# Gates of chunks 1 to 5 on 80 partitions, with the running maximum copied there by DMA

## The chip, the cores and the metric

The kernel runs on one core of a Trainium2 chip. The core has a matrix engine (TensorE, PE in the profile, with weight loads shown as PEld), a vector engine (VectorE, DVE), an engine for activation functions (ScalarE, ACT), a general engine (GpSimd, POOL) and a queue processor (SyncE, SP) that issues the DMA transfers here. The engines run side by side and wait for one another through semaphores. The metric is the time of one execution on the device in microseconds (us); less is better.

## The reference

Three layers follow one another: a gated linear attention with a stabilised recurrence, a feed-forward layer with a smooth relu, and a soft mixture of eight experts whose weights are normalised in eight rounds. The change lies in the gates of the first:

```python
for t in range(S):                                   # S = 768, for each of 2 batches and 8 heads
    m_new = maximum(f_gate[t] + m, i_gate[t])        # running maximum, m starts at -1e30
    f_stab = exp(f_gate[t] + m - m_new)
    i_stab = exp(i_gate[t] - m_new)
    m = m_new
    C = f_stab * C + i_stab * outer(v[t], k[t])
    n = f_stab * n + i_stab * k[t]
    h = C @ q[t];  nq = n . q[t]
    y[t] = sigmoid(o_gate[t]) * h / max(|nq|, 1)
# x = y as 1536 tokens x 320
# layer 2: g = smooth relu of x @ w_in (320 x 2048); x = g @ w_out
# layer 3: P = exp(x @ w_gate - max), 8 rounds of row and column normalisation;
#          out = sum over 8 experts of P[:, e] * (relu(x @ w1[e]) @ w2[e])
```

All is float32; the kernel splits operands into a high and a low part for the matrix engine.

## The kernel before

The sequence is cut into 6 chunks of 128 tokens; with 2 batches there are 12 attention tiles, tile t being chunk t // 2 of batch t % 2. Within a chunk the recurrence is written as matrices. For that the gates are needed in three forms: the stabilised f along the tokens (G, spread to all 128 partitions), the stabilised i and the running product of f by token (gt), and each chunk's whole product (lend).

The gates stand in one tile g_all on 32 partitions (batch and head, held twice), with i, f and the running maximum m along 768 columns. `gate_exps(a, b)` makes the running maximum by one scan (line 306), then f + m - m_new (309, 310) and i - m_new (312) on DVE and the exponentials on ACT (311, 313). It is called for columns 0 to 128 and then for 128 to 768. `gate_prods` makes the running product with one scan for each chunk (325); for chunk 0 it also makes g_s (318 to 322), from which PE spreads the first tiles' gates to all partitions (375). For chunks 1 to 5 it writes f to a scratch g_d in HBM in four transfers (332), from which `load_g` loads G for one tile, broadcast to 128 partitions (144). `gate_by_token` transposes i and the product by PE (339, 340) into gt (341); `gate_ends` makes lend (345 to 353).

`attn(t)` is a generator. It multiplies v by i (364, POOL), makes scores on PE (378), a scan that builds decay factors from G (382) and their product with the scores, A (384, DVE), the product of A with the values (399, PE) and with the earlier state (394), the state update (387, 406, 411, 439), and the division: den (427 to 429) and sg (431, 432) on DVE. Three transposes (445) and a split (112, 114) bring the result to XH and XL, the input of layer 2. Tiles 0 and 1 run as a pair first; `warm` puts filler matmuls on a dummy tile wz between their steps (295). The rest runs inside layer 2's first block of 512 tokens.

Layer 2's weights come as 64-bit floats and are decoded on DVE (212, 213, 216, 219) after an absolute value on ACT (211), then split (234 and 235, 242 to 247, 252 to 255). `PUMP` says at which steps of the first pair a piece is started. Four buffers (raw) hold loaded pieces. In layer 2, line 123 multiplies x by w_in into a bank, 538 to 544 apply the smooth relu and split it into XH and XL again, and 554 to 558 multiply by w_out. Layer 3 does the same with lines 123, 703, 704 and 684 to 686.

The order in which each engine runs its instructions is made by the framework's scheduler when the program is built, from the order in the code and its own estimates; on the chip each engine, and SP with its transfers, then goes through a fixed list. `GP = 8` is the step of the first pair at which `gates_rest` (the gates of chunks 1 to 5, and their loads) is written into the program. A transfer also waits until the eighth transfer before it has landed, since eight semaphores take turns.

Of the kernel before, what the change touches and what calls it, by code (L numbers as in the profile page):

```python
# [8 lines left out]
F32 = mybir.dt.float32  # L9
# [16 lines left out]
C_ID, C_ND, C_N16, C_M16, C_PM, C_W = 0, 160, 162, 163, 179, 187  # L26
C_TOT = 291
# [9 lines left out]
GP = 8  # L37
# [9 lines left out]
def mlstm_moe_moe_kernel(  # L47
# [77 lines left out]
    with ExitStack() as atx:  # L125
# [156 lines left out]
        zer = cst[0:32, 32 : 32 + L]  # L282
        m16_r = ap.tile([32, 16], F32R, name="m16_r")
# [31 lines left out]
        def gate_prods(c0, c1):

            if c0 == 0:
                act(out=g_s, in_=g_f[:, 0:L], func=ACTF.Copy)
                vec.scalar_tensor_tensor(
                    out=g_s, in0=f(g_s), scalar=cst[0:32, C_N16 : C_N16 + 1], in1=g_f[:, 0:L], op0=ALU.mult, op1=ALU.add,  # L320
                )
                vec.tensor_copy(g_s[:, 0:1], zer[:, 0:1])
            for c in range(c0, c1):
                cs = slice(c * L, (c + 1) * L)
# [459 lines left out]
```

## Time and profile before

| | before |
|---|---|
| median of 3 runs | 1002.05 us (1001.83 to 1002.8) |
| the profiled execution | 1001.51 us, span 999.7 us |
| PE busy | 985.7 us (99%) |
| DVE busy | 468.8 us (47%) |
| ACT busy | 346.1 us (35%) |
| POOL busy | 34.0 us (3%) |
| mean DMA rate | 52 GB/s |
| chain that ended last | PE 85%, DVE 9%, ACT 2%, issue 2%, DMA 2% |

The shares are means over stages of different kinds. From about 125 us on, PE multiplies almost without a pause (layers 2 and 3). The first 125 us hold the attention, the decoding of weights and the first block of layer 2, and there DVE is busy nine tenths or more in nearly every slice. Part of what counts as PE's busy time there is filler. The chain of work that ended last runs through DVE's instructions in that stretch and through PE's afterwards.

### The profile page before, as it was taken

The numbers are of one execution on the slowest core, as the hardware profiler recorded it, in microseconds if no ns is written. First come the engines' busy times: TensorE is split into PE (matmuls) and PEld (weight loads), VectorE is DVE, ScalarE is ACT, GpSimd is POOL, SyncE is SP. The second block draws the span as 40 slices with busy tenths as digits, with TensorE's granted clock in tenths as the row PEclk, the third lists the DMA queues.
The fourth block names the chain that finished last, engine by engine and source line by source line (L and its number), as shares of the span: only waits on it lengthen the run. The fifth ranks groups of instructions, "written<-read, shape, count | busy, mean of one in ns | idle before, by whom it ended". The sixth has DMA issues, their size and how long they took to land.

```text
span 999.7 us, 13739 instructions
## 1 busy us (share of the span) xinstructions
PE 985.7 (99%) x5648; PEld 874.0 (87%) x5664; DVE 468.8 (47%) x854; ACT 346.1 (35%) x624; POOL 34.0 (3%) x43
## 2 busy tenths in 40 slices
PE   9989999999999999999999999999999999999998
PEld 5778999887887899999999999999999998999997
DVE  9989977644464553422522432252243234222222
ACT  3645746556784223211411321231132113111111
POOL 2221111000000000000000000000000000000000
PEclk9989999999999999999999999999999999999999
DMA  6954342100133001200300210030021002000000
GB/s 170 265 163 124 120 126 75 35 1 1 30 103 100 1 1 42 75 1 1 116 1 1 58 59 1 1 116 1 1 74 43 1 12 76 1 1 1 27 27 27
DMA packets 42191, 51.93 MB, mean 52 GB/s; under 512 B 3360, under 2 KB 35744, under 8 KB 42128
## 3 DMA queue, kind: packets, MB, share of 16 engines
q1 hardware_dynamic: 42128, 51.05, 17.5%
q8 instruction: 44, 0.72, 0.3%
q14 instruction: 19, 0.16, 0.1%
HBM read 49.03 MB, written 2.01 MB: 51 GB/s over the span
## 4 chain that ended last, share of the span: by engine, by line
PE 85%; DVE 9%; ACT 2%; issue 2%; DMA 2%; SPq 0%; DVEq 0%; ACTq 0%
PE bk_g L123 41%; PE bk_g L684 8%; PE bk_g L686 8%; PE bk_g L685 8%; PE bk_ax L685 3%; PE bk_ax L684 3%; PE bk_ax L686 3%; PE bk_at L399 2%; PE bk_g L555 1%; PE bk_g L556 1%; PE bk_g L554 1%; PE bk_at L378 1%; DMA raw<-in_w_dram 1%; DVE dv L216 1%; PE bk_g L558 1%
## 5 line engine op out<-in xcount | busy, mean ns | idle before, releaser
L123 PE MATMUL bk_g<-XH,wk 128*128 128x512 f32 (+1 forms) x1280 | 404.1, 383 | 0.8 <-ACT XH L112 0.6
L704 DVE SCALAR_TENSOR_TENSOR lo<-bk_g,hi 128x512 fp32r<-128x512 f32 x192 | 132.6, 691 | 375.0 <-ACT hi L703 374.1
L123 PE MATMUL bk_g<-XL,wk 128*128 128x512 f32 (+1 forms) x768 | 288.7, 377 | 0.2 <-DVE XL L114 0.2
L123 PEld LDWEIGHTS bk_g<-XH,wk 128*128 128x128 f32 x1280 | 236.2, 188 | 43.6 <-ACT XH L112 1.0
L703 ACT ACTIVATE hi<-bk_g 128x512 fp32r<-128x512 f32 x192 | 114.9, 599 | 449.6 <-PE bk_g L123 449.2
L684 PE MATMUL bk_g<-wf,hi 128*128 128x320 f32 x576 | 177.4, 308 | 0.8 <-ACT hi L703 0.8
L685 PE MATMUL bk_g<-wf,hi 128*128 128x320 f32 x576 | 177.0, 307 | 0.0
L686 PE MATMUL bk_g<-wf,lo 128*128 128x320 f32 x576 | 176.9, 308 | 0.0
L123 PEld LDWEIGHTS bk_g<-XL,wk 128*128 128x128 f32 x768 | 144.6, 188 | 21.1 <-DVE XL L114 0.4
L684 PEld LDWEIGHTS bk_g<-wf,hi 128*128 128x128 f32 x576 | 108.0, 187 | 7.8 <-ACT hi L703 1.2
L685 PEld LDWEIGHTS bk_g<-wf,hi 128*128 128x128 f32 x576 | 108.0, 188 | 6.3
L686 PEld LDWEIGHTS bk_g<-wf,lo 128*128 128x128 f32 x576 | 107.9, 187 | 0.0
L685 PE MATMUL bk_ax<-wf,hi 128*128 128x320 f32 x192 | 59.1, 308 | 0.0
L684 PE MATMUL bk_ax<-wf,hi 128*128 128x320 f32 x192 | 59.0, 307 | 0.0
L686 PE MATMUL bk_ax<-wf,lo 128*128 128x320 f32 x192 | 58.4, 304 | 0.0
L538 ACT ACTIVATE gs<-bk_g 128x512 f32<-128x512 f32 x48 | 28.5, 593 | 40.9 <-PE bk_g L123 40.8
L718 DVE SCALAR_TENSOR_TENSOR acc<-bk_g,P,acc 128x320 f32<-128x320 f32 x63 | 30.8, 545 | 15.3 <-PE bk_g L686 15.3
L542 DVE TENSOR_TENSOR gs<-bk_g,gs 128x512 f32<-128x512 f32 x32 | 22.1, 690 | 33.8 <-ACT gs L540 33.8
L686 PEld LDWEIGHTS bk_ax<-wf,lo 128*128 128x128 f32 x192 | 36.0, 188 | 0.0
L684 PEld LDWEIGHTS bk_ax<-wf,hi 128*128 128x128 f32 x192 | 36.0, 188 | 0.0
L685 PEld LDWEIGHTS bk_ax<-wf,hi 128*128 128x128 f32 x192 | 35.9, 187 | 0.0
L530 DVE TENSOR_TENSOR wf<-raw,wf 128x640 fp32r<-128x640 f32 x32 | 26.3, 826 | 15.5 <-ACT wf L529 15.3
(194 smaller groups left out, 1040.1 us busy)
## 6 DMA issues: line engine op xcount, KB each, us to landing
raw<-in_w_dram SPq DMA_DIRECT2D x32, 320.0 KB
raw<-in_w_dram SPq DMA_DIRECT2D x32, 256.0 KB
kvo_t<-in_kvo_dram SPq DMA_DIRECT2D x12, 484.0 KB
raw<-in_w_out_dram SPq DMA_DIRECT2D x8, 640.0 KB
raw<-in_w_in_dram SPq DMA_DIRECT2D x8, 512.0 KB
raw<-in_w_dram SPq DMA_DIRECT2D x64, 64.0 KB
qk<-in_qk_dram SPq DMA_DIRECT2D x24, 160.0 KB
G<-g_d SPq DMA_DIRECT2D x5, 512.0 KB
```

The costliest lines, as they stand in the source:

```text
L123: mm(dst, a, b, start=i == 0, stop=i == len(seq) - 1)
L216: vec.scalar_tensor_tensor(out=v_i, in0=lo_i, scalar=29, in1=v_i, op0=ALU.logical_shift_right, op1=ALU.bitwise_or,)
L399: mm(pa[:, h * 41 : (h + 1) * 41], A[h % 2][:, h // 2, :], vw[:, h, :], start=True, stop=True)
L530: vec.tensor_tensor(out=wf[:, fs, 320:640], in0=rs[n], in1=f(wf[:, fs, 0:320]), op=ALU.subtract)
L538: act(out=t, in_=pg, func=ACTF.Relu, scale=-1.0, bias=1.0)
L542: vec.tensor_tensor(out=g, in0=pg, in1=t, op=ALU.max)
L684: mm(pp[i], hi[:, ts], wf[:, ff, 0:320], start=st, stop=False)
L685: mm(pp[i], hi[:, ts], wf[:, ff, 320:640], start=False, stop=False)
L686: mm(pp[i], lo[:, ts], wf[:, ff, 0:320], start=False, stop=sp)
L703: act(out=hi, in_=pg, func=ACTF.Relu)
L704: vec.scalar_tensor_tensor(out=lo, in0=pg, scalar=0.0, in1=f(hi), op0=ALU.max, op1=ALU.subtract)
L718: vec.scalar_tensor_tensor(out=acc[:, t, :], in0=pp[i], scalar=P[:, t, e : e + 1], in1=acc[:, t, :], op0=ALU.mult, op1=ALU.add)
```

## The change

The running maximum is still made on 32 partitions over all 768 columns. For chunks 1 to 5 everything after it is done on a new tile gl with 80 partitions, one for each chunk and head (16 of them a chunk), and 128 columns. Its f and i are loaded straight from HBM by ten transfers of 16 partitions; the running maximum is copied to gl_m by five transfers of 16 x 129, from SBUF to SBUF. The three tensor-tensor steps, two exponentials and one product scan then run once on 80 x 128. The scratch g_d has one row for each chunk and head and is written by one transfer of 80 x 128; G is loaded in two halves of four heads. The ten transposes become two of 80 columns; the ends come from a product with a constant table on 80 rows. Chunk 0 keeps its own path, with its product in g_p. `GP` goes from 8 to 2.

```diff
-GP = 8
+GP = 2
...
-        g_d = dram.tile([16, S - L], F32, name="g_d")
+        NLR = (NCH - 1) * 16
+        g_d = dram.tile([NLR, L], F32, name="g_d")
...
+        gl = ap.tile([NLR, 3, L + 1], F32, name="gl")
+        gl_i, gl_f, gl_p = (gl[:, i, 0:L] for i in range(3))
+        gl_m = ap.tile([NLR, L + 1], F32, name="gl_m")
+        for x, o in ((gl_f, S), (gl_i, 0)):
+            for c in range(1, NCH):
+                nc.sync.dma_start(x[(c - 1) * 16 : c * 16], gates[0:16, o + c * L : o + (c + 1) * L])
...
-            nc.sync.dma_start(
-                G1 if t % 2 else G0, g_d[b * 8 : b * 8 + 8, (c - 1) * L : c * L].unsqueeze(0).to_broadcast([128, 8, L])
-            )
+            g, r = G1 if t % 2 else G0, (c - 1) * 16 + b * 8
+            for hf in range(2):
+                nc.sync.dma_start(
+                    g[:, hf * 4 : hf * 4 + 4, :], g_d[r + hf : r + 7 + hf : 2, :].unsqueeze(0).to_broadcast([128, 4, L])
+                )
...
         def gates_rest():
-            gate_prods(1, NCH)
-            gate_by_token(1, NCH)
-            gate_ends()
+            gates_later()
...
+        def gates_first():
+
+            gate_max(0, L)
+            gate_exps(g_f[:, 0:L], g_i[:, 0:L], g_m[:, 0:L], g_m[:, 1 : L + 1])
+            act(out=g_s, in_=g_f[:, 0:L], func=ACTF.Copy)
...
+            vec.tensor_tensor_scan(out=g_p, data0=g_f[0:16, 0:L], data1=zer[0:16], initial=1.0, op0=ALU.mult, op1=ALU.add)
...
+            gate_max(L, S)
+            for c in range(1, NCH):
+                nc.sync.dma_start(gl_m[(c - 1) * 16 : c * 16], g_m[0:16, c * L : (c + 1) * L + 1])
+
+        def gates_later():
+            gate_exps(gl_f, gl_i, gl_m[:, 0:L], gl_m[:, 1 : L + 1])
+            vec.tensor_tensor_scan(out=gl_p, data0=gl_f, data1=cst[0:NLR, C_Z : C_Z + 1].to_broadcast([NLR, L]), initial=1.0, op0=ALU.mult, op1=ALU.add)
+            gp.tensor_copy(gl_f[:, 0:1], cst[0:NLR, C_Z : C_Z + 1])
+            nc.sync.dma_start(g_d, gl_f)
+            p = bank("g1")
+            nc.tensor.transpose(p[:, 0:NLR], gl_i, ident[0:NLR, 0:NLR])
+            nc.tensor.transpose(p[:, NLR : 2 * NLR], gl_p, ident[0:NLR, 0:NLR])
...
+            vec.tensor_scalar(
+                out=z, in0=cst[0:NLR, C_PM : C_PM + (NCH - 1) * 8], scalar1=gl_p[:, L - 1 : L], scalar2=None, op0=ALU.mult,
+            )
```

`gate_max` is the scan of line 306 and `gate_exps` the five steps after it.

The scheduler's order moves with it. On SP, at the start of the program, the loads of tiles 0 and 1 (qk, kvo_t), of the first weights (raw) and the writes of g_d stood so before:

```order
L138 DMA cst<-in_consts_dram 128x291
L161 DMA qk_94<-in_qk_dram 40x1024
L161 DMA qk_94<-in_qk_dram 40x2x512
L162 DMA kvo_t<-in_kvo_dram 128x968
L161 DMA qk_95<-in_qk_dram 40x1024
L161 DMA qk_95<-in_qk_dram 40x2x512
L162 DMA kvo_t<-in_kvo_dram 128x968
L194 DMA raw<-in_w_in_dram 128x1024 x2
L198 DMA raw<-in_w_in_dram 64x1024 x2
L201 DMA raw<-in_w_out_dram 128x2x640
L332 DMA g_d<-g_all 4x640
```

and now:

```order
L140 DMA cst<-in_consts_dram 128x323
L147 DMA gl<-in_gates_dram 16x128 x10
L170 DMA qk_106<-in_qk_dram 40x1024
L170 DMA qk_106<-in_qk_dram 40x2x512
L171 DMA kvo_t<-in_kvo_dram 128x968
L170 DMA qk_107<-in_qk_dram 40x1024
L170 DMA qk_107<-in_qk_dram 40x2x512
L171 DMA kvo_t<-in_kvo_dram 128x968
L342 DMA gl_m<-g_all 16x129 x5
L203 DMA raw<-in_w_in_dram 128x1024 x2
L207 DMA raw<-in_w_in_dram 64x1024
L348 DMA g_d<-gl 80x128
```

The loads of the tiles stand behind ten more transfers, the first weights behind fifteen, and the write of g_d has moved ahead of the last two weight loads of the first five (L207 and L210 follow it).

On DVE, where the first two tiles' scans and products meet the first decoding (dv, raw), the list was before (id is a constant table, scr the second tile's G and A):

```order
L382 SCALAR_TENSOR_TENSOR scr<-bk_g_180,id_116 128x512
L345 TENSOR_TENSOR z<-g_all,cst 16x48
L384 TENSOR_TENSOR scr<-bk_g_185,scr 128x512
L382 SCALAR_TENSOR_TENSOR G_90<-bk_at,id_116 128x512
L384 TENSOR_TENSOR A<-bk_at,G_90 128x512
L212 TENSOR_SCALAR dv<-dv 128x512
L213 TENSOR_SCALAR dv<-dv 128x512
L382 SCALAR_TENSOR_TENSOR scr<-bk_g_234,id_116 128x512
L216 SCALAR_TENSOR_TENSOR dv<-raw,dv 128x512
```

and now ends so, from tile 1's last product to the first decode steps:

```order
L393 TENSOR_TENSOR scr<-bk_g_269,scr 128x512
L436 TENSOR_SCALAR den<-bk_at 128x8
L437 TENSOR_TENSOR den<-bk_at,den 128x8
L320 TENSOR_TENSOR gl<-gl,gl_m 80x128
...
L440 TENSOR_TENSOR sg<-bk_g_328,sg 128x320
L438 RECIPROCAL den<-den 128x8
L346 SCALAR_TENSOR_TENSOR gl<-gl,cst 80x128
L441 TENSOR_TENSOR sg<-sg,den 128x320
L357 TENSOR_SCALAR z<-cst,gl 80x40
L221 TENSOR_SCALAR dv<-dv 128x512
L222 TENSOR_SCALAR dv<-dv 128x512
```

The first decode step stood among the scans and products of tiles 0 and 1; it now stands behind the last step of both tiles' division and of the later gates. On PE the numbers of fillers between the first steps change: 22 of them, the two transposes of chunk 0 and 3 more fillers come ahead of the first fan-out of g_s (L384, before L375), which is now made for both tiles at once; then 16 fillers, the first scores (L387, before L378), the second fan-out, scores, 9 fillers, and scores, fan-out and scores of tile 1. Before, the first fan-out, the first scores and tile 1's fan-out followed one another with no filler between.

## Rows read from the trace of the kernel before

**Rows 1.** Stretches: us, busy PE, PEld, DVE, ACT, POOL, clock, DMA share, GB/s

```profile
20.00:30.00 10.00, 9.89 (x71) 7.51 (x72) 10.00 (x21) 4.67 (x9) 1.03 (x1) 1.00 0.40 118
80.00:100.00 20.00, 19.64 (x159) 18.46 (x160) 19.46 (x34) 11.10 (x22) 3.05 (x4) 1.00 0.44 126
100.00:125.00 25.00, 24.19 (x194) 22.59 (x196) 24.19 (x49) 17.94 (x34) 3.27 (x3) 1.00 0.40 120
```

**Rows 2.** Instructions on tile g_all: count, ns min/median/max, first and last start

```profile
L325 DVE TENSOR_TENSOR_SCAN g_all<-g_all,cst x6: 385/395/413, 8.2 to 14.0; 32x128 f32<-32x128 f32 x6
...
L309 DVE TENSOR_TENSOR g_all<-g_all x2: 278/544/811, 5.3 to 7.5; 32x128 f32<-32x128 f32 x1, 32x640 f32<-32x640 f32 x1
L312 DVE TENSOR_TENSOR g_all<-g_all x2: 273/776/1280, 5.5 to 9.6; 32x128 f32<-32x128 f32 x1, 32x640 f32<-32x640 f32 x1
L310 DVE TENSOR_TENSOR g_all<-g_all x2: 272/538/804, 5.7 to 8.8; 32x128 f32<-32x128 f32 x1, 32x640 f32<-32x640 f32 x1
```

**Rows 3.** SP in order of time: start us, us of issuing, line, transfer

```profile
2.13 1.35 SPq L161 DMA_DIRECT2D qk<-in_qk_dram  x2
...
8.11 0.47 SPq L201 DMA_DIRECT2D raw<-in_w_out_dram  x1
14.70 0.65 SPq L332 DMA_DIRECT2D g_d<-g_all  x1
```

**Rows 4.** PE in order of time: start us, us, line, operation, count

```profile
8.21 0.23 PE L339 MATMUL bk_g<-cst,g_all 16*128 16x16 f32 x1
...
10.10 0.66 PE L375 MATMUL bk_at<-g_s,m_r 32*128 32x128 f32 x4
10.69 1.16 PE L378 MATMUL bk_at<-qk 104*128 104x128 f32 x8
...
24.32 1.87 PE L399 MATMUL bk_g<-vw,scr 128*128 128x41 f32 x16
...
29.19 2.77 PE L295 MATMUL bk_g<-wz 128*128 128x512 bf16 x12
```

**Rows 5.** DVE in order of time, same columns

```profile
18.12 0.45 DVE L212 TENSOR_SCALAR dv<-dv 128x512 f32<-128x512 f32 x1
...
18.95 1.22 DVE L382 TENSOR_TENSOR_SCAN scr<-bk_g,id 128x512 f32<-128x512 f32 x1
...
22.48 0.68 DVE L384 TENSOR_TENSOR scr<-bk_g,scr 128x512 f32<-128x512 f32 x1
...
28.33 0.16 DVE L428 TENSOR_TENSOR den<-bk_at,den 128x8 f32<-128x8 f32 x1
...
31.53 0.44 DVE L431 TENSOR_TENSOR sg<-bk_at,sg 128x320 f32<-128x320 f32 x1
...
32.00 0.49 DVE L432 TENSOR_TENSOR sg<-sg,den 128x320 f32<-128x320 f32 x1
```

**Rows 6.** Stretches of 4 us (columns as rows 1), then PE's waits in brackets

```profile
48.00:52.00 4.00, 4.00 (x35) 3.74 (x34) 2.58 (x9) 3.23 (x7) 0.00 (x0) 1.00 1.06 258
...
64.00:68.00 4.00, 2.04 (x10) 1.69 (x12) 4.00 (x9) 2.14 (x5) 0.00 (x0) 0.90 0.62 162
68.00:72.00 4.00, 4.00 (x22) 4.00 (x22) 1.57 (x4) 1.22 (x2) 0.00 (x0) 0.50 0.91 294
72.00:76.00 4.00, 4.00 (x21) 4.00 (x21) 2.98 (x9) 0.26 (x1) 0.90 (x1) 0.50 0.68 176
76.00:80.00 4.00, 3.22 (x19) 2.77 (x19) 3.67 (x6) 2.03 (x4) 0.00 (x0) 0.82 0.51 139
...
44.77 1.03 PE L295 MATMUL bk_at<-wz 128*128 128x512 bf16 x3 [1.01 <-DVE A L384]
...
65.63 0.50 PE L554 MATMUL bk_g<-XH,wf 128*128 128x256 f32 x2 [3.66 <-ACT XH L543]
```

**Rows 7.** ACT in order of time, same columns as rows 4

```profile
11.66 1.28 ACT L401 ACT_TABLE_LOAD   x1
12.96 0.83 ACT L401 ACTIVATE sg<-kvo_t 128x320 f32<-128x320 f32 x2
```

More of the change, by code (lines that the diff above doesn't have):

```diff
@@ L25 @@
 EF = 1024
[L26 to L27 removed]
+C_ID, C_ND, C_N16, C_M16, C_PM, C_W = 0, 160, 162, 163, 179, 219
+C_Z = 161
+C_TOT = 323
 NGS, NHL = 2, 5
@@ L282, in mlstm_moe_moe_kernel @@
         zer = cst[0:32, 32 : 32 + L]
+        g_p = ap.tile([16, L], F32, name="g_p")
         m16_r = ap.tile([32, 16], F32R, name="m16_r")
@@ L315, in gate_prods @@
[L315 to L324, printed above, removed]
-                vec.tensor_tensor_scan(out=g_m[:, cs], data0=g_f[:, cs], data1=zer, initial=1.0, op0=ALU.mult, op1=ALU.add)
-            if c0:
-                gp.tensor_copy(
-                    g_f[:, c0 * L : c1 * L].rearrange("p (c t) -> p c t", t=L)[:, :, 0:1], zer[:, 0 : c1 - c0].unsqueeze(2)
-                )
-                for j in range(4):
-                    o = j // 2 * 8 + j % 2
-                    nc.sync.dma_start(g_d[j * 4 : j * 4 + 4, :], g_f[o : o + 7 : 2, L:S])
@@ L334, in gate_by_token, with gate_exps @@
-        def gate_by_token(c0, c1):
-            p = bank("g1")
-            for c in range(c0, c1):
-                cs = slice(c * L, (c + 1) * L)
-                o = (c - c0) * 32
-                nc.tensor.transpose(p[:, o : o + 16], g_i[0:16, cs], ident[0:16, 0:16])
-                nc.tensor.transpose(p[:, o + 16 : o + 32], g_m[0:16, cs], ident[0:16, 0:16])
-            act(out=gt[:, c0:c1, :], in_=p[:, 0 : 32 * (c1 - c0)].rearrange("p (c e) -> p c e", e=32), func=ACTF.Copy)
-        def gate_ends():
-            z = ap.tile([16, NCH, 8], F32, name="z")
-            vec.tensor_tensor(
-                out=z,
-                in0=g_m[0:16, 0:S].rearrange("p (c t) -> p c t", t=L)[:, :, L - 1 : L].to_broadcast([16, NCH, 8]),
-                in1=cst[0:16, C_PM : C_PM + 8].unsqueeze(1).to_broadcast([16, NCH, 8]),
-                op=ALU.mult,
+        def gate_exps(fg, ig, m, m_new):
+            vec.tensor_tensor(out=fg, in0=fg, in1=m, op=ALU.add)
+            vec.tensor_tensor(out=fg, in0=fg, in1=m_new, op=ALU.subtract)
+            act(out=fg, in_=fg, func=ACTF.Exp)
+            vec.tensor_tensor(out=ig, in0=ig, in1=m_new, op=ALU.subtract)
+            act(out=ig, in_=ig, func=ACTF.Exp)
@@ new lines, in gates_later @@
+        def gates_later():
[6 more added lines that the diff above has]
+            nc.tensor.transpose(p[:, NLR : 2 * NLR], gl_p, ident[0:NLR, 0:NLR])
+            act(
+                out=gt[:, 1:NCH, :].rearrange("p c (w r) -> p w c r", w=2),
+                in_=p[:, 0 : 2 * NLR].rearrange("p (w c r) -> p w c r", w=2, r=16), func=ACTF.Copy,
+            )
+            z = ap.tile([NLR, (NCH - 1) * 8], F32, name="z")
+            vec.tensor_scalar(
+                out=z, in0=cst[0:NLR, C_PM : C_PM + (NCH - 1) * 8], scalar1=gl_p[:, L - 1 : L], scalar2=None, op0=ALU.mult,
@@ L350, in gate_ends @@
             )
             p = bank("g1")
-            mm(p[0:104, 0 : NCH * 8], cst[0:16, C_W : C_W + 104], z.rearrange("p c e -> p (c e)"), start=True, stop=True)
-            act(out=lend, in_=p[0:104, 0 : NCH * 8], func=ACTF.Copy)
+            mm(p[0:104, 0 : (NCH - 1) * 8], cst[0:NLR, C_W : C_W + 104], z, start=True, stop=True)
+            act(out=lend[:, 8 : NCH * 8], in_=p[0:104, 0 : (NCH - 1) * 8], func=ACTF.Copy)
         def attn(t, tags):
@@ L735, in _consts @@
         c[r, C_M16 + r % 16] = 1.0
-    for r in range(16):
-        c[r, C_PM + r // 2] = 1.0
+    for r in range((NCH - 1) * 16):
+        c[r, C_PM + r // 16 * 8 + r % 16 // 2] = 1.0
         c[r, C_W + (r % 2) * 64 : C_W + 64 + (r % 2) * 40] = 1.0
```

21 lines of the change are left out of this document (9 added, 12 removed).

## The prediction

> **What bounds the kernel now.** I read the stretches first. From 80 us on TensorE (PE) is all but full: it idles 0.36 us of 80 to 100 and 0.81 of 100 to 125 [rows 1], and the page gives it 99% of the span. The change touches none of that work, so what it can do lies before about 125 us. There VectorE (DVE) is the full engine: 10.00 of 10 us in 20 to 30, 19.46 of 20 and 24.19 of 25 later [rows 1], while PE is kept busy partly by filler matmuls on a dummy tile. So the first question is when DVE gets through its part, and the second whether PE's waits for DVE make its clock fall.
>
> Both show in the stretch from 60 us. PE sits idle for 3.66 us until ScalarE's XH comes, which follows a DVE instruction; then the granted clock reads 0.90, 0.50, 0.50 and 0.82 of full in four stretches of 4 us, that is 1.2 instead of 2.4 GHz for 0.8 + 4.0 + 4.0 + 1.4 = 10.2 us, and half of that, 5.1 us of PE's work, is lost [rows 6]. A gap of 1.01 us at 44.77 had no such sequel [rows 6]. DVE in turn waits for the slow PE: 2.43 + 1.02 + 0.33 = 3.8 us of 68 to 80 [rows 6].
>
> **What DVE is spared.** Removed are the three wide tensor-tensor steps over 640 columns, 0.81 + 0.80 + 1.28 = 2.89 us, and the six scans of 128 columns, 6 x 0.395 = 2.37 us, together 5.26 us [rows 2]. Added are the same three steps over 128 columns on 80 partitions, priced by the same lines' short form, 3 x 0.28 = 0.83 us, and two scans (one for chunk 0 on 16 partitions, one for the rest on 80), 2 x 0.40 = 0.79 us [rows 2]. More partitions at the same number of columns I take to be free: the 128x512 step of line 384 lasts 0.68 us [rows 5], 1.3 ns a column, and the 32x640 step of line 309 with 0.81 us 1.3 as well. The product z has its counterpart. DVE saves 5.26 - 1.62 = 3.6 us. ScalarE's two exponentials also shrink, but they wait for other engines there and are worth nothing.
>
> **What the order takes away.** The order of the changed kernel matters more than the sizes. In the old one, decoding of weights (lines 212 to 219 and 235) stands among the scans and products of the first two attention tiles and begins at 18.12 us [rows 5]. In the new one all of it stands behind the den, sg and gate steps of both tiles. What these wait for is PE, whose order also changed. I follow it with old durations. PE reaches the first two small transposes at 8.21 us as before [rows 4], then come three fillers at 2.77/12 = 0.23 us and eight fan-out matmuls (0.66 us for four): 10.5 us. Sixteen fillers follow, 3.7 us, so the first scores (line 378, now 387) start near 14.1 instead of 10.69 us [rows 4]. Four scores cost 1.1, the second fan-out 0.6, four more scores 1.1: 17.0. Nine fillers are 2.1, the scores and fan-outs of tile 1 another 2.8: 21.9. The product with the values takes 1.7 us net for tile 0, four fillers 0.9, and tile 1's product then starts at about 24.5, where it started at 24.32 before [rows 4]. The attention itself is thus not late, but not early either, and ends near 26.3.
>
> DVE can do nothing else meanwhile. In the old kernel it ran from 18.12 to 28.33 us without a gap and gave this time to decoding except for one scan (1.22), one product (0.68) and a den step: about 8.2 us of decoding [rows 5]. In the new one tile 1's den, sg (0.16 or so three times, 0.44, 0.49), the 80-partition scan (0.40), tile 0's last sg step (0.49) and z follow the value product at 26.3, so decoding starts near 28.5 with none done. What it has done instead is the den and sg work of both tiles, 2 x (3 x 0.16 + 0.44 + 0.49) = 2.8 us [rows 5], which the old kernel still has before it at 28.33. DVE is behind by 8.2 - 2.8 = **5.4 us** there, the 3.6 us saved already counted: its idle time up to this point has grown by about 9 us.
>
> **The queue of SP.** Fifteen more transfers are issued early, ten for the gates and five for the running maximum. Old issues last 0.47 us (128 x 2 x 640) to 0.68 us (half of 1.35, two of 40 partitions) [rows 3], so at 0.47 to 0.68 us each the ten push the loads of q, k and v back by 4.7 to 6.8 us, and the five push the first weight loads by 2.4 to 3.4 more. I take the lower end, because the rows copied are short. The scores at 14.1 us hide this: the old loads of tile 0 were issued from 2.13 us and used at 10.69 [rows 3, 4], the new ones are issued from about 7 and used 7 us later. Weights issued near 14 are wanted at 28. What is not hidden so well is the single write of the scratch g_d, at its place in the queue ahead of the fourth and fifth weight loads: it waits for the 80-partition scan, near 28 us, where the old first write of g_d stood at 14.70 [rows 3]. Those weights can land near 31 (an estimate: 28, issues of 0.5 to 0.7 us [rows 3] and about 2 us under way) and are wanted when two other pieces are decoded, about 33. This costs 0 to 2 us; I take 0. The loads of G become 20 issues instead of 10, in a queue that then waits for buffers anyway.
>
> **ScalarE.** Exponentials of the later chunks now stand after the first sigmoids, so there are two more table loads, 1.28 us each, after which the sigmoids start within 0.02 us [rows 7]. The first lies in a wait. The second stands between two steps of the first relu piece, whose result DVE takes late anyway. Cover: DVE's lag of over 4 us; if that were gone it would cost 1.3 us. The Trainium skill, "ScalarE: Activation LUTs", section "What ACT_TABLE_LOAD costs", puts each switch at about 2.66 us, since it adds a drain of about 1.38 us. The row after the load shows no such gap. By the page ScalarE would lose an estimated 5.3 instead of 2.6 us, and the sum would move by at most the second drain.
>
> **The sum.** DVE's lag of 5.4 us at 28 us can shrink where the old DVE itself waited for others. From 48 to 52 us it was busy 2.58 of 4 us [rows 6]; with DVE late, these 1.4 us go. That leaves 5.4 - 1.4 = 4.0 us when the second group of relu results is made (64 us before). Behind it, PE waits for XH as before, its clock falls once, in the old place or after an earlier gap, and from 80 us there is no slack on either engine [rows 1]. The 4.0 us arrive at the end. The profiled execution took 1001.51 us (span 999.7), the median of the runs is 1002.05, half a microsecond more and within what runs differ by. With it: 1002.05 + 4.0 = 1006.0 us.
>
> **Rivals.**
> *The lag is worked off.* DVE's 3.8 us of waiting from 68 to 80 us depend on the slow PE. If a late DVE finds PE's results there already, the lag shrinks to 4.0 - 3.8 = 0.2 us: 1002.3 us; half of it gives 1004. For it: PE's order runs partly ahead. Against: that wait came of the clock, which fell because DVE was late; a later DVE does not help the clock.
> *Faster.* The long gap before 65.63 us splits in two short ones, like that of 1.01 us at 44.77, after neither of which the clock falls [rows 6]. Then 5.1 us come back: 1006.0 - 5.1 = 1000.9, and with part of the 3.8 us of DVE's waits also gone, 998 to 1000. This decides if no idle stretch of PE before 80 us is much over 1 us. For it: the place of the gap is set by the order of a few instructions. Against: the gap that ended at 44.77 us was a wait for DVE. In the new order PE waits there for the first relu piece's XH, which hangs on DVE too; with DVE 4.0 to 5.4 us late the gap grows from 1.01 to some 5 us, unless PE is late itself.
> *Two falls of the clock.* If the gap near 45 us brings one and the later gap stays, another 5.1 us are lost: 1011 us. Against: a slow PE would arrive late at the second gap and fill it.
>
> **How the numbers follow.** A difference below 0.2%, 2 us, can hardly be told from no change here. I give the lag as summed (1004.1 to 1008) 0.50, the lag worked off (1000.1 to 1004) 0.26, faster 0.13, two falls 0.11. Hence slower 0.61, same 0.26, faster 0.13. The range reaches from 1001.0, where the lag is all but gone, to 1011.0, one more fall; it leaves out faster and about 0.05 beyond the top.
>
> **What would show it.** Right: in the new profile DVE is well below full from 10 to 28 us, its first decode step stands near 28 us, PE's first scores near 14, and its waits for ScalarE's XH are followed by one stretch at half clock. The step on SP is wrong if scores or weights wait for transfers. The order argument is wrong if DVE's idle time before 28 us is below 4 us. The forecast fails, with that part right, if the half-clock stretch is gone or doubled.

## The result: slower by 1.4%, more than three times as far as forecast

| | before | after |
|---|---|---|
| median | 1000.85 us (999.26 to 1002.80, 6 runs) | 1015.63 us (1009.37 to 1020.38, 6 runs) |
| ratio | | 1.0136 [1.0109, 1.0163] |
| the profiled execution | 1001.51 us, span 999.7 | 1013.58 us, span 1011.8 |
| mean granted clock of that span | 0.995 | 0.987 |
| DVE busy | 468.8 us | 465.8 us |

The forecast was 1006.0 us, with 1011 as its upper end. The direction was right and the size was not: the medians differ by 14.8 us and the profiled executions by 12.1, where the sum said 4.0. The readings below explain the 12.1. DVE is spared 3.0 us, and the kernel is slower all the same.

The early part of the program went as the prediction followed it. From the timelines of the kernel after, in order of time: PE's first scores and its product with the values for tile 1, DVE's first decoding step, and SP's issues (start us, us, line, operation, count).

```profile
13.29 0.94 PE L387 MATMUL bk_at<-qk 104*128 104x128 f32 x7
...
23.63 1.87 PE L408 MATMUL bk_g<-vw,scr 128*128 128x41 f32 x16
```

```profile
27.43 0.41 DVE L221 TENSOR_SCALAR dv<-dv 128x512 f32<-128x512 f32 x1
```

```profile
2.11 4.59 SPq L147 DMA_DIRECT2D gl<-in_gates_dram  x10
...
10.55 3.15 SPq L342 DMA_DIRECT2D gl_m<-g_all  x5
13.75 1.23 SPq L203 DMA_DIRECT2D raw<-in_w_in_dram  x2
...
27.92 0.33 SPq L348 DMA_DIRECT2D g_d<-gl  x1
```

Decoding begins at 27.43 us, where it began at 18.12 [rows 5]. The stretches of after that answer to [rows 1, 6] (us, busy PE, PEld, DVE, ACT, POOL, clock, DMA share, GB/s):

```profile
20.00:30.00 10.00, 9.92 (x80) 8.42 (x81) 7.64 (x23) 3.43 (x12) 1.59 (x2) 1.00 0.07 18
...
48.00:52.00 4.00, 2.09 (x7) 0.95 (x8) 4.00 (x7) 1.53 (x4) 1.44 (x2) 0.66 1.09 329
52.00:56.00 4.00, 4.00 (x18) 3.43 (x16) 2.14 (x5) 1.26 (x2) 0.00 (x0) 0.50 1.07 342
...
72.00:76.00 4.00, 1.01 (x3) 0.71 (x3) 4.00 (x10) 2.83 (x6) 0.00 (x0) 0.65 0.46 134
76.00:80.00 4.00, 3.83 (x17) 3.46 (x18) 1.46 (x4) 0.95 (x2) 0.00 (x0) 0.50 0.92 286
...
100.00:125.00 25.00, 25.00 (x205) 23.60 (x204) 24.66 (x49) 17.84 (x33) 1.53 (x2) 1.00 0.47 150
```

The clock now falls to half (1.2 GHz) twice, near 49 and near 74 us, where [rows 6] show one fall; a shorter third fall, near 155 us, comes up below. PE's long waits ahead of both (the releaser in brackets) are:

```profile
48.59 0.50 PE L560 MATMUL bk_g<-XH,wf 128*128 128x256 f32 x2 [4.16 <-ACT XH L549]
...
74.04 0.79 PE L560 MATMUL bk_g<-XH,wf 128*128 128x256 f32 x2 [3.46 <-ACT XH L549]
```

**What a fall costs is to be read on DVE, a few microseconds later.** DVE is the full engine here, and after a fall it waits for PE's slow products. These are all of its waits over 1 us between 28 and 100 us, of before and then of after:

```profile
71.43 0.50 DVE L422 TENSOR_TENSOR hv<-hv,bk_at 128x328 f32<-128x328 f32 x1 [2.36 <-PE bk_at L399]
72.96 0.32 DVE L439 TENSOR_TENSOR Cst<-bk_at,Cst 40x164 f32<-40x164 f32 x1 [1.03 <-PE bk_at L406]
```

```profile
56.57 0.49 DVE L431 TENSOR_TENSOR hv<-hv,bk_at 128x328 f32<-128x328 f32 x1 [2.44 <-PE bk_at L408]
63.39 0.56 DVE L115 TENSOR_TENSOR XL<-bk_ax,XH 128x384 fp32r<-128x384 f32 x1 [1.10 <-ACT XH L113]
...
80.51 0.50 DVE L431 TENSOR_TENSOR hv<-hv,bk_at 128x328 f32<-128x328 f32 x1 [3.06 <-PE bk_at L408]
87.26 0.56 DVE L115 TENSOR_TENSOR XL<-bk_ax,XH 128x384 fp32r<-128x384 f32 x1 [1.06 <-ACT XH L113]
```

Before, 2.36 + 1.03 = 3.39 us; after, 2.44 + 1.10 + 3.06 + 1.06 = 7.66. With two falls DVE waits 4.3 us more; that the two waits for ACT (1.10 and 1.06) come of the falls too is read from their place only. All of DVE's idle time from 28 to 100 us, short waits too, was 72 - 66.20 = 5.8 us and is now 72 - 62.77 = 9.2 (before, then after; columns as above):

```profile
28.00:100.00 72.00, 65.29 (x460) 57.49 (x466) 66.20 (x125) 39.23 (x79) 14.60 (x12) 0.93 0.63 182
```

```profile
28.00:100.00 72.00, 59.77 (x383) 51.86 (x382) 62.77 (x116) 37.45 (x75) 10.02 (x12) 0.83 0.63 190
```

**A second new loss lies near 150 us.** DVE's list of after, from one relu step to the next input of layer 2, the wait of PE that goes with it, and the stretch:

```profile
150.49 0.70 DVE L548 TENSOR_TENSOR bk_g<-bk_g,gs 128x512 f32<-128x512 f32 x1 [0.68 <-ACT gs L546]
151.23 1.66 DVE L391 TENSOR_TENSOR_SCAN g_all<-g_all,id 128x512 f32<-128x512 f32 x1
152.82 0.66 DVE L393 TENSOR_TENSOR A<-bk_at,g_all 128x512 f32<-128x512 f32 x1
153.40 0.67 DVE L550 TENSOR_TENSOR XL<-bk_g,XH 128x512 fp32r<-128x512 f32 x1
```

```profile
153.53 1.79 PE L408 MATMUL bk_at<-vw,A 128*128 128x41 f32 x14 [1.51 <-DVE A L393]
```

```profile
150.00:160.00 10.00, 8.49 (x57) 7.62 (x56) 6.92 (x12) 2.38 (x6) 0.73 (x1) 0.83 0.22 68
```

The scan of the first half of tile 11's G (in g_all) stands ahead of A, the product of tile 9's second half, for which PE waits 1.51 us, and the clock of this stretch is 0.83. Before, the same relu step, marked by the same 0.68 us of waiting, starts at 141.91, A follows it directly at 142.51, and 150 to 160 us has clock 1.00:

```profile
141.91 0.70 DVE L542 TENSOR_TENSOR bk_g<-bk_g,gs 128x512 f32<-128x512 f32 x1 [0.68 <-ACT gs L540]
142.51 0.68 DVE L384 TENSOR_TENSOR A<-bk_at,g_all 128x512 f32<-128x512 f32 x1
```

SP's issues of that tile's loads show why the scan can stand so early (after, then before):

```profile
147.39 0.36 SPq L155 DMA_DIRECT2D g_all<-g_d  x1
153.50 0.37 SPq L155 DMA_DIRECT2D g_all<-g_d  x1
```

```profile
143.74 0.43 SPq L144 DMA_DIRECT2D g_all<-g_d  x1
```

With halves, the first half is loaded when tile 9's first product has been made (it starts at 146.68 and lasts 0.68 us), and its scan no longer has to follow the second product at 152.82. Before, the one load came behind both products, and the first scan at 150.78.

That relu step is the marker in what follows. The end of this coupled part is the first matmul of layer 3 (the first start of line 684, now 690): 304.0 us before, 315.3 after (the time ahead of "to" in each row):

```profile
L684 PE MATMUL bk_g<-wf,hi x75: 307/308/417, 304.0 to 398.3; 128*128 128x320 f32 x75
```

```profile
L690 PE MATMUL bk_g<-wf,hi x66: 304/308/415, 315.3 to 398.9; 128*128 128x320 f32 x66
```

Behind it both kernels need about the same (695.7 and 696.5 us to the end of the span).

### The profile page after: what moved, and what is told of

It reads as the page before. It is cut to its first block, busy times and chain, and to the rows that moved or that the text cites. A ratio compares the mean times of both kernels' runs of the same rounds, so it can differ in the third digit from the quotient of the medians.

```text
span 1011.8 us, 13779 instructions
## 1 busy us (share of the span) xinstructions
PE 990.6 (98%) x5656; PEld 879.2 (87%) x5656; DVE 465.8 (46%) x850; ACT 346.7 (34%) x626; POOL 28.1 (3%) x43
## 4 chain that ended last, share of the span: by engine, by line
PE 87%; DVE 7%; ACT 2%; DMA 2%; issue 1%; SPq 0%; POOL 0%; DVEq 0%; ACTq 0%
PE bk_g L124 40%; PE bk_g L690 8%; PE bk_g L692 8%; PE bk_g L691 8%; PE bk_ax L690 3%; PE bk_ax L691 3%; PE bk_ax L692 3%; PE bk_at L408 2%; PE bk_g L305 2%; PE bk_g L561 1%; PE bk_g L562 1%; PE bk_g L560 1%; PE bk_at L387 1%; DMA raw<-in_w_dram 1%; DVE dv L225 1%
## 5 line engine op out<-in xcount | busy, mean ns | idle before, releaser
L544 ACT ACTIVATE gs<-bk_g 128x512 f32<-128x512 f32 x48 | 28.5, 593 | 35.9 <-PE bk_g L124 35.9
L305 PE MATMUL bk_g<-wz 128*128 128x512 bf16 x114 | 33.0, 413 | 3.4 <-DVE XL L550 2.5
```

The lines of the kernel that those rows point to most:

```text
L305: mm(to, wz, wz[:, 0:1].to_broadcast([128, 512]), start=True, stop=True)
L544: act(out=t, in_=pg, func=ACTF.Relu, scale=-1.0, bias=1.0)
```

## The experiments

Each run was timed beside the kernel before on the same chip; the ratio is to that, with its 95% interval. The rival theories were: DVE's lag at 28 us, grown on the way (lag); the clock's falls (clock); the early transfers on SP (transfers); the changed `GP`; the extra table loads. G in halves was suspected only when these were done, so the earlier expectations don't speak of it. "id4", "wz" and "pp" in the edits are a constant table, the filler tile and layer 2's output banks.

### What a lag costs

Before, with one, three or five idle scans of 128x512 on DVE behind tile 1's last product (1.2, 3.6, 6.1 us):

```diff
+                for _ in range(N if t == 1 and hf else 0):
+                    vec.tensor_tensor_scan(out=lagt, data0=A[hf].rearrange("p h t -> p (h t)"), data1=id4, initial=0.0, op0=ALU.mult, op1=ALU.add)
```

> The kernel before with one extra scan of 128x512 on VectorE (1.2 us, its result unused) behind the last product of tile 1, near 23 us. Theory of a lag that arrives one to one at the end: 1003.2 us. [...] Theory that this lag is worked off: 1001 to 1002.

> The kernel before with three extra scans of 128x512 there (3.6 us). One to one: 1005.6 us. [...] Worked off, or the loss of the changed kernel not from VectorE's lag: 1001 to 1004.

> The kernel before with five extra scans of 128x512 on VectorE (6.1 us) behind tile 1's last product. One to one: 1007.5 us. Lag 3.6 us gave +4.8 us (lag3) and 1.2 us gave -1.7 (lag1), so from these the lag of 6.1 gives +7 to +9, 1008.5 to 1010.5. If a lag of this size alone makes the changed kernel's loss: 1012 to 1017.

Measured: 0.9983 [0.9970, 0.9996], 1.0048 [1.0029, 1.0067] and 1.0073 [1.0047, 1.0100], that is -1.7, +4.8 and +7.3 us. A lag of 3.6 or 6.1 us arrives at the end with about a microsecond more; it is not multiplied.

Both traces show a second stretch at half clock all the same, although G is loaded whole there: lag3 from 48 and from 68 us, lag5 from 40 and from 72 us. Added up from stretches of 4 us as in the prediction, the time at half clock between 28 and 172 us is 10.2 us before, 17.1 in lag3, 20.5 in lag5 and 27.4 in after. In lag5 DVE is idle from 28 to 100 us as long as in after, 9.2 us, and the relu step that is the marker comes at 150.06, where after has 150.49:

```profile
28.00:100.00 72.00, 60.65 (x396) 52.59 (x402) 62.77 (x119) 34.47 (x71) 10.58 (x12) 0.86 0.59 169
```

So a late DVE is enough for a second fall and for its waits. With one scan the kernel even gains. Its PE and DVE rows show how:

```profile
65.75 3.21 PE L403 MATMUL bk_at<-vw,A 128*128 128x41 f32 x14 [3.61 <-DVE A L386]
```

```profile
70.52 0.32 DVE L443 TENSOR_TENSOR Cst<-bk_at,Cst 40x164 f32<-40x164 f32 x1 [1.15 <-PE bk_at L410]
...
139.20 0.70 DVE L546 TENSOR_TENSOR bk_g<-bk_g,gs 128x512 f32<-128x512 f32 x1 [0.68 <-ACT gs L544]
```

The long wait of PE now stands ahead of another product, DVE waits 1.15 instead of 3.39 us behind it, and the marker comes 2.7 us earlier although DVE has 1.2 us more to do.

### Small rivals

`GP` at 8 in the changed kernel, and at 2 in the old one (one line each):

> The changed kernel with GP back at 8, so that the later gates are made behind more of the first tiles' work in the program; in VectorE's order the first decode step still stands behind all den and sg steps of both tiles. Theory 1 (order): no gain, 1011 to 1020 us. Theories 2 and 3: the same 1011 to 1020. Theory 4 (the gates stand too early): back to 1000 to 1006.

> The kernel before with GP = 2 alone, the old gates on 32 partitions. By it decoding stands a little earlier than before in VectorE's order, with 640-column steps and scans ahead of it as before. Theory 1 (order): the same as before within 3 us, 998 to 1004 us. Theories 2 and 3: the same. Theory 4 (gates too early): 1008 to 1016.

Measured: 1.0146 [1.0109, 1.0184], as slow as after, with decoding still late. In the old kernel `GP = 2` alone costs 0.8%, 1.0079 [1.0060, 1.0099]: the order that it gives leaves waits of PE of 2.92 and 4.62 us at 48.74 and 71.28. So `GP` is no part of the loss in the changed kernel that could be told here, though the old gates do not bear its change.

The sigmoid of tiles 0 and 1 replaced by Exp, so that no table is exchanged there (the output gate of these tiles is left out):

```diff
-            act(out=sg[:, 0:320], in_=kvo_t[:, 648:968], func=ACTF.Sigmoid)
+            act(out=sg[:, 0:320], in_=kvo_t[:, 648:968], func=ACTF.Exp if t < 2 else ACTF.Sigmoid)
```

> The changed kernel with Exp in the place of Sigmoid for tiles 0 and 1, which leaves the output gate of these two tiles out; the two extra table loads on ScalarE are gone, one of them between two steps of the first relu piece. VectorE's order stays late (decoding behind the den steps of tile 1's first). Order theory: 1009 to 1016 us, at most 2 us better than the changed kernel. Rival (the table loads delay XH, and TensorE's gaps and falls follow from that): 1000 to 1006.

Measured: 1.0119 [1.0082, 1.0157], not to be told from after; the interval leaves room for a price of a few microseconds either way. In after the sigmoid follows its load at once:

```profile
42.35 1.28 ACT L410 ACT_TABLE_LOAD   x1
43.64 0.47 ACT L410 ACTIVATE sg<-kvo_t 128x320 f32<-128x320 f32 x1
```

The load ends at 43.63. The further drain that the Trainium skill, "ScalarE: Activation LUTs", section "What ACT_TABLE_LOAD costs", puts into the price does not show between these two rows.

The first two weight loads ahead of the five copies of the running maximum:

```diff
+        rs0 = [m1_load(*x) for x in M1SEQ[0:2]]      # right after the loads of tiles 0 and 1
...
-            rs = [m1_load(*x) for x in M1SEQ[0:2]]
+            rs = rs0
```

> The changed kernel with the first two weight loads issued right behind the tile loads, ahead of the five small transfers of gl_m on SP. Nothing else is edited; all fifteen small transfers, the 80-partition gates and the two extra table loads stay. By it the first decode step on VectorE stands behind tile 0's first den step instead of behind all den and sg steps of both tiles. Theory 1 (the order puts decoding late, VectorE idles, TensorE then waits for XH and its clock falls two or three times): decoding begins near 23 to 24 us instead of 27.4, VectorE's lag at the first relu piece shrinks by 2 to 4 us, the gaps of TensorE before the first pieces shrink, at least one stretch at half clock goes: 1003 to 1010 us. Theory 2 (the fifteen transfers themselves delay what is loaded): 1012 to 1018. Theory 3 (the two table loads or the 80-partition steps in ScalarE's queue): 1012 to 1018. Theory 4 (the gates stand too early, GP = 2): 1012 to 1018.

Measured: 1.0108 [1.0080, 1.0137]. DVE's idle time before 28 us shrinks from 10.5 to 9.2 only, so the five copies are a small part of it.

All fifteen transfers issued by GpSimd instead of SP (`nc.sync.dma_start` becomes `gp.dma_start`):

> The changed kernel with the ten loads of gl and the five copies of gl_m issued by GpSimd instead of SP. By it VectorE's order comes near that of the kernel before: the first two weight pieces are decoded ahead of the last product of tile 1. Theory 1 (order): decoding begins at 18 to 20 us, the gap of 4.2 us at 48 us shrinks below 2 us, one stretch at half clock at most is left: 996 to 1003 us. Theory 2 (the transfers themselves, by any queue): 1010 to 1018. Theories 3 (table loads) and 4 (gates at GP = 2): 1012 to 1018.

Measured: 1.0148 [1.0127, 1.0169], and inconclusive on the queue. The order did become early, but then DVE waited for the copies in the middle of its early work; from DVE's timeline and the page's part on DMA issues (last column: median us from issue to landing):

```profile
19.00 0.29 DVE L320 TENSOR_TENSOR gl<-gl,gl_m 80x128 f32<-80x128 f32 x1 [3.93 <-DMA gl_m<-g_all]
```

```profile
gl_m<-g_all POOLq DMA_DIRECT2D x5, 8.1 KB, 6.7
```

### The clock's falls

The old kernel with 24 fillers (zeros, added to the bank) put into PE's long wait of 3.66 us [rows 6], so that PE isn't idle there:

```diff
+                for i in range(24):      # ahead of the third 256-wide product with w_out
+                    mm(pp[0], wz, wz[:, 0:1].to_broadcast([128, w]), start=False, stop=False)
```

> The kernel before with 24 such fillers ahead of the third piece's wait for XH (65.6 us), nothing else. Clock theory: the one stretch at half clock is gone, its 5.1 us come back in part or whole, 995.5 to 999 us. Rival (half clock lies under VectorE's work): 1000 to 1003.

Measured: 0.9992 [0.9976, 1.0008], with the clock at 1.00 throughout. Taking the fall away wins 0.9 us, within what can't be told from nothing. The trace shows a gain that is given back (DVE's marker; then all of PE's waits in this stretch up to layer 3):

```profile
138.75 0.70 DVE L543 TENSOR_TENSOR bk_g<-bk_g,gs 128x512 f32<-128x512 f32 x1 [0.68 <-ACT gs L541]
```

```profile
295.21 0.50 PE L564 MATMUL bk_g<-hi,wf 128*128 128x512 f32 x1 [0.42 <-ACT hi L544]
295.94 0.50 PE L565 MATMUL bk_g<-lo,wf 128*128 128x512 f32 x1 [0.23 <-DVE lo L545]
302.86 0.41 PE L694 MATMUL bk_g<-wf,hi 128*128 128x320 f32 x1 [1.38 <-ACT hi L713]
```

The marker comes 3.2 us earlier than before, about the 3.39 us of DVE's waits that are gone. Then PE waits 0.42 + 0.23 + 1.38 = 2.0 us at the end of layer 2, where before it waited 0.8, and layer 3 begins at 302.9 against 304.0.

The changed kernel with fillers in both waits, in two versions (24 and 24 small ones, the first group behind a step on ACT; then 10 in float32 and 44):

> The changed kernel with 24 filler matmuls (128x256, of zeros, added into a bank of the sum) right ahead of the instruction that waits for the first relu piece's XH (48.6 us in the profile after) and 24 ahead of the third piece's (74.0 us); those of the first piece use a second zero tile that ScalarE writes from the second piece's bank, so that they stand late. The order of the rest stays. Clock theory (waiting makes TensorE's clock fall, and half clock costs about 13.7 us in the profile after): both stretches at half clock there are gone, 1003 to 1008 us, what is left is VectorE's lag. Rival (VectorE bounds this stretch anyway, half clock lies under its work): 1012 to 1018.

> The changed kernel with ten filler matmuls of zeros (32x128 by 32x256, f32) ahead of the first piece's wait for XH and 44 (128x256, bf16) ahead of the third piece's, more than in fill_a and without its extra ScalarE step; TensorE's order behind them shifts a little. After fill_b, where the clock stayed full and the time did not move, I expect that the clock is worth little here too while VectorE lags. VectorE theory: time at half clock falls below 14 us, the result stays at 1009 to 1016. Clock theory: 1001 to 1007.

Measured: 1.0126 [1.0097, 1.0155] for the first, inconclusive: its first group waited itself for ACT until 51.14, the fall near 50 us is gone, but there is one from about 23 to 33 us that after doesn't have, and the one behind 75 us stayed. The second gave 1.0113 [1.0091, 1.0134], with a mean clock of 0.997; the interval overlaps that of after, so a gain in time isn't shown. Its trace shows what the falls do to DVE: with 6.8 us at half clock between 28 and 172 us instead of 27.4, DVE's waits shrink to one of 1.20 us, its idle time from 28 to 100 us falls from 9.2 to 4.2, the marker comes at 147.77 instead of 150.49, and layer 3 begins at 311.7 instead of 315.3. What is left is the place near 150, where PE waits for A as in after (the scan ahead of it waited 1.89 us for its load):

```profile
149.08 2.27 PE L409 MATMUL bk_at<-vw,A 128*128 128x41 f32 x14 [2.11 <-DVE A L394]
```

### The early transfers

The loads of tiles 0 and 1 first, then the two weight loads, then the ten loads of gl (late_gl); and the same with gl loaded by one transfer from a copy of the gates laid out by chunk in HBM (one_gl):

```diff
-        for x, o in ((gl_f, S), (gl_i, 0)):
-            for c in range(1, NCH):
-                nc.sync.dma_start(x[(c - 1) * 16 : c * 16], gates[0:16, o + c * L : o + (c + 1) * L])
...
+        rs0 = [m1_load(*x) for x in M1SEQ[0:2]]      # right after the loads of tiles 0 and 1
+        for x, o in ((gl_f, S), (gl_i, 0)):          # late_gl: the ten loads
+            for c in range(1, NCH):
+                nc.sync.dma_start(x[(c - 1) * 16 : c * 16], gates[0:16, o + c * L : o + (c + 1) * L])
+        nc.sync.dma_start(gl[:, 0:2, 0:L], gates2)   # one_gl: in place of these ten
```

> The changed kernel with the first two weight loads and then the ten loads of gl issued behind the tile loads on SP (tiles, two weights, ten gl, five gl_m); nothing else is edited. By it VectorE's order has the first decode steps ahead of tile 1's last scan again, as in the kernel before, with the 80-partition steps behind. Order theory (VectorE's idle time before 28 us builds the loss, whatever the clock does): decoding begins near 18 to 20 us, VectorE's idle time before 28 us falls from 10.5 to 3 to 6 us, 1000 to 1006 us. Rival (the small transfers or the 80-partition gates themselves cost it): 1010 to 1018.

> As late_gl, but the ten loads of gl are one: the host lays the gates of chunks 1 to 5 out on 80 rows as well. SP issues six small transfers instead of fifteen. Order theory: as late_gl or up to 2 us better, 999 to 1005 us. Rival (the number of small transfers on SP): clearly better than late_gl, by 4 us or more. Rival (the 80-partition gates themselves): 1010 to 1018.

Measured: 1.0054 [1.0034, 1.0074] and 1.0067 [1.0045, 1.0088]. With `GP = 8` they are the same, 1.0047 [1.0027, 1.0067] and 1.0066 [1.0044, 1.0087]:

> late_gl with GP back at 8: the small transfers behind the tile loads and the first weights, and the later gates made behind more of the first tiles' work. In VectorE's order the 80-partition steps stand behind tile 1's den steps. Theory (two separate losses, the place of the transfers and the place of the gates in the program): the remaining 5.4 us shrink to 0 to 3, 999 to 1004 us. Rival (what is left is the 80-partition gates and their chain by themselves, or chance of the order): 1005 to 1009.

> one_gl (one load of gl instead of ten, behind the tile loads and the first weights) with GP back at 8. In VectorE's order the 80-partition steps are spread among the decoding of the third and fourth weight pieces. Theory of two losses: 997 to 1003 us; if VectorE's 3 us of saved work get through, below the kernel before. Rival: 1005 to 1009.

In late_gl decoding begins at 17.03 us, among the attention again, DVE's idle time before 28 us is 5.9 us, not 10.5, and no wait of DVE behind a slow PE is over 1 us. It gives back 8.2 us of the 13.6, with 17.0 us at half clock between 28 and 172 us.

### G loaded whole

The changed kernel with G loaded in one transfer a tile as before. For that the scratch is written with the heads in the order of G (two transfers instead of one); all else stays:

```diff
-            for hf in range(2):
-                nc.sync.dma_start(
-                    g[:, hf * 4 : hf * 4 + 4, :], g_d[r + hf : r + 7 + hf : 2, :].unsqueeze(0).to_broadcast([128, 4, L])
-                )
+            nc.sync.dma_start(g, g_d[r : r + 8, :].unsqueeze(0).to_broadcast([128, 8, L]))
...
-            nc.sync.dma_start(g_d, gl_f)
+            for hf in range(2):
+                nc.sync.dma_start(g_d.rearrange("(u r i) t -> u r i t", r=2, i=4)[:, hf], gl_f[hf : NLR : 2])
```

> The changed kernel with the tiles of G loaded whole, as before: g_d is written in two transfers that sort the rows by parity of the head, and each tile is read by one transfer instead of two. VectorE's order near 150 us becomes that of the kernel before (tile 11's first scan behind tile 9's last product), the order before 28 us stays that of the changed kernel. Theory (the halves cost a wait near 150 us and the half clock that follows it): TensorE's wait of 1.51 us at 153.5 falls to 0.3 or less, the half-clock stretch of 154 to 160 us goes, 1009 to 1013 us, 3 to 5 us better than the changed kernel. Rival (that wait costs nothing, TensorE has slack there): 1014 to 1018.

Measured: 1005.97 us (1005.65 to 1006.15), ratio 1.0053 [1.0032, 1.0074]: better than was expected of this run, and as it happens next to the prediction's 1006.0. In this order the halves cost 0.8%. DVE's idle time before 28 us is unchanged (10.3), and the clock is not back to one fall: it falls in three places, near 41, 52 and 72 us, with 13.7 us at half clock in all. But DVE waits for the slow PE once, its idle time from 28 to 100 us is 5.0 us instead of 9.2, and near 150 us A stands directly behind the relu step again, while PE hardly waits and the clock is full:

```profile
77.50 0.32 DVE L446 TENSOR_TENSOR Cst<-bk_at,Cst 40x164 f32<-40x164 f32 x1 [1.48 <-PE bk_at L413]
...
146.43 0.70 DVE L546 TENSOR_TENSOR bk_g<-bk_g,gs 128x512 f32<-128x512 f32 x1 [0.68 <-ACT gs L544]
147.04 0.68 DVE L391 TENSOR_TENSOR A<-bk_at,g_all 128x512 f32<-128x512 f32 x1
147.79 0.69 DVE L548 TENSOR_TENSOR XL<-bk_g,XH 128x512 fp32r<-128x512 f32 x1
```

```profile
150.00:160.00 10.00, 9.95 (x85) 9.84 (x85) 6.97 (x14) 5.41 (x11) 2.42 (x2) 1.00 0.32 109
```

Whole G together with late_gl and with one_gl:

> late_gl (transfers of gl behind the tiles and the first weights) and whole tiles of G. Theory of two places (transfers early, 8.2 us; halves of G, 3 to 5 us): 1001 to 1004 us, near the kernel before. Rival (the rest is something else): 1005.5 to 1008, as late_gl.

> one_gl and whole tiles of G; VectorE has about 3 us less work than in the kernel before and no extra wait that I know of. Theory of two places: 999.5 to 1003.5 us; below the kernel before if the saved work gets through. Rival: 1006 to 1009, as one_gl.

Measured: 1.0052 [1.0031, 1.0074] for the first, so the two gains of about 8 us don't add: whole G, worth 0.8% in after's order, changes nothing in that of late_gl (1.0054). Its trace has a new wait and a new fall of its own (PE, then the stretch):

```profile
129.62 0.58 PE L559 MATMUL bk_g<-XH,wf 128*128 128x256 f32 x1 [2.45 <-ACT XH L548]
```

```profile
130.00:140.00 10.00, 10.00 (x60) 9.54 (x61) 7.54 (x15) 2.40 (x5) 1.51 (x2) 0.68 0.26 88
```

At clock 0.68 this stretch alone loses 3.2 us of PE's work. The second, with a single load of gl, takes 997.38 us (996.53 to 1002.07, 12 runs), ratio 0.9969 [0.9956, 0.9983]: **faster than both kernels.** Its profiled execution, 1002.07 us, was the slowest of the twelve (the others took 996.5 to 998.2), so its rows do not show where the median's gain lies.

The traces side by side (us):

| | before | after | whole_g | late_gl | one_whole |
|---|---|---|---|---|---|
| DVE idle before 28 | 2.0 | 10.5 | 10.3 | 5.9 | 7.2 |
| DVE's waits for PE or XH over 1 us, 28 to 100 | 3.39 | 7.66 | 1.48 | 0 | 5.18 |
| DVE idle, 28 to 100 | 5.8 | 9.2 | 5.0 | 5.7 | 6.6 |
| at half clock, 28 to 172 | 10.2 | 27.4 | 13.7 | 17.0 | 13.7 |
| marker, relu step near 145 | 141.9 | 150.5 | 146.4 | 143.9 | 143.0 |
| marker to layer 3 | 162.1 | 164.8 | 161.6 | 164.7 | 160.9 |
| first matmul of layer 3 | 304.0 | 315.3 | 308.0 | 308.6 | 303.9 |

The line "marker to layer 3" sets the halves apart: 163.7 to 166.1 us in the kernels with halves (164.5 and 164.0 in rawfirst and one_gl), against 160.9 to 162.5 in those with G whole (lag1, lag3, lag5 and late_whole among them). Two don't fit: gp8, with halves, has 162.7, and fill_b, with G whole, 164.1, of which 1.2 are the waits from 295 us on shown above.

## Why the prediction was too low

**The order and the lag: right.** First scores 13.29 us (forecast 14.1), tile 1's value product 23.63 (24.5), first decoding 27.43 (28.5). DVE's idle time before 28 us has grown by 8.5; less the 3.0 us of work that it is spared (forecast 3.6) DVE is behind by 5.5 us, where the sum said 5.4.

**What of the lag is worked off: right where it was read, wrong over the whole stretch.** From 48 to 52 us DVE is now full, 4.00 of 4 us against 2.58 [rows 6], the 1.4 us that the sum took off. But from 28 to 100 us its idle time has not shrunk by 1.4 us, it has grown by 3.4 (5.8 to 9.2), for the reason given under the fall of the clock.

**SP's queue and the write of g_d: right where they were costed in time of issue.** An issue lasts 0.46 us for gl (4.59 / 10) and 0.63 for gl_m (3.15 / 5), the write stands at 27.92, and PE's scores did not come late. But late_gl, with the ten loads moved, gets decoding back among the attention and wins 8.2 us. The transfers cost PE and DVE nothing by waiting (neither waits for one in after before 100 us); the order of DVE that they entail costs, and the sum had this already in its 5.4.

**Table loads: right** as far as no_sig can tell.

**The one fall of the clock: the step that failed first.** The sum let the clock fall "once, in the old place or after an earlier gap", and the rival of two falls was held unlikely since "a slow PE would arrive late at the second gap and fill it". It did not: in place of the gap of 1.01 us near 45 us there is one of 4.16, as the prediction itself worked out for the case that PE is not late, and 3.46 us of the second one remained. So the rival with two falls, given 0.11, named what happened, and the prediction's own sign of failure, a doubled stretch at half clock, is there. It priced the second fall by PE's 5.1 us; DVE's long waits grew by 4.3 and its idle time from 28 to 100 us by 3.4, where the sum had -1.4. Up to the marker DVE is either busy or idle, so its delay splits without a rest: 8.5 us more idle time before 28 us, 3.4 more from 28 to 100, as much as before from there to the marker, and 3.4 us less work. That is about the 8.6 us measured; the sum had about 9, -1.4 and 3.6, together 4.0. That the falls cause this idle time is shown by fill_a2, where with 6.8 us at half clock left it drops to 4.2 us; fill_b shows the same in the old kernel (3.4 us instead of 5.8).

**"The loads of G become 20 issues instead of 10": the second step, a term at 0 that was not 0.** The prediction priced the issues, and these cost nothing. What it did not ask is what else hangs on a transfer's size. DVE scans G half by half in every kernel here; with a load for each half, the first half's scan depends on its own load only, and the scheduler places it ahead of a product that PE waits for. From the marker to layer 3 that is 164.8 - 162.1 = 2.7 us, in a part that the sum held to be without slack by rows that end at 125 us. With the 8.6 this makes the 11.3 us by which layer 3 begins later.

**What whole_g shows, and what not.** With G whole the marker is 4.1 us earlier and the way from it to layer 3 is 3.2 us shorter. The second part is tied to the halves by the rows above. The first is not: lag5 has the second fall and the same 9.2 us of idle time with G whole, so a late DVE brings them by itself, and whole_g has more than one fall too, only placed so that DVE waits 1.48 us behind them. In after the first relu piece's step stands at 46.96 on DVE and in whole_g at 45.15, behind fewer decoding steps, and PE's wait near 50 us is 2.18 instead of 4.16: the halves changed this order too, and the cost of a fall depends on it. That whole_g lands next to 1006.0 us is therefore in part luck; its path, several falls with few waits, is not that of the sum, and against the kernel before timed beside it (1000.77 us) it is 5.2 us slower, not 4.0.

**The price of a fall: wrong in kind.** The rival "faster" let 5.1 us of PE's work come back if the fall went. fill_b took the fall away: 3.2 us came back at the marker, about 1 was left where layer 3 begins, and the measured time moved by 0.9 us, which can't be told from none. In this stretch DVE sets the pace, so a fall costs what DVE waits behind it, and not what PE loses; late_gl, with 17.0 us at half clock, has no such wait over 1 us. The Trainium skill, "TensorE: Matmul & The Clock Gate", section "Terms", prices the throttled time of PE at its full loss, half of it at half clock; that is the 5.1 us of before [rows 6], and the measurement of fill_b does not bear it out for a stretch where another engine is the full one.

Open is how the single load of gl brings another 8 us together with whole G, when alone it is no better than ten loads (1.0067 and 1.0054). All these kernels do nearly the same work in other orders, and their times lie between 997 and 1017 us. So whether the order alone, by chance of the scheduler, or a part of the change sets a given time stays open, and a separate share for each part can't be given from such sums. Open too is the spread of after's own runs, 1009 to 1020 us: the mean granted clock goes with it (0.990 at 1009.37, 0.978 at 1020.38), while whole_g's four runs lie within 0.5 us at 0.993 to 0.995; which of the two leads was not tried. The traces of two relatives give a hint: no_sig (profiled at 1019.06 us, its other runs took 1011.4 to 1011.9) and fill_a (1015.74) have a further stretch at half clock from about 23 to 33 us, with DVE waiting 2.65 and 3.40 us behind it, though PE shows no wait over 0.3 us from 10 to 23 us; after's trace has none. That this makes after's spread is not shown.

## What to carry to other kernels

When an edit changes the size of a transfer, look at what consumes it: halves let the scheduler place the consumer's halves apart, and a first half that moves ahead of what another engine waits for can cost most of what the change was to win (2.7 us here, where DVE was spared 3.0). Price a fall of the clock by the waits of the engine that sets the pace behind it, and count PE's long waits one by one rather than assuming that one fall excludes the next. Where several in-order engines hand work to one another without slack, try a change in two or three orders: here three more edits (the loads of gl later, as one transfer, and G whole) turned 1.4% slower into 0.3% faster.

## What the hardware did that was not expected

- Taking away the whole stretch at half clock (10 us, 5.1 us of PE's work) left the time as it was: 0.9992 [0.9976, 1.0008] in fill_b.
- 1.2 us more work on DVE made the old kernel faster by 0.17% (0.9983 [0.9970, 0.9996] in lag1), with the order of the instructions behind it changed.
- Copies of 16 x 129 floats from SBUF to SBUF, issued by GpSimd, landed a median of 6.7 us after their issue (allpool), long enough to stall the engine that was to be helped.
- Small transfers are not cheaper to issue in proportion: 8 KB took SP 0.46 us and one of 16 x 129 from SBUF 0.63, against 0.47 for 640 KB [rows 3].
